# A convolution spectrum's opening in one fixed order of pieces on all engines

## The chip, the core and the metric

The kernel runs on one core of a Trainium2 chip. The metric is the device time of one execution in microseconds, taken as the median over the runs. A core has TensorE (matrix products), VectorE, ScalarE and GpSimd (elementwise work and copies), SyncE (which mainly issues transfers), and 16 DMA engines that move data. Each engine works through its own instructions in order and waits on semaphores. In the profile's lines the engines are PE, DVE, ACT, POOL and SP; PEld is TensorE's loading of stationary operands, and a "q" behind an engine's name is its queue of issued instructions.

## What is computed

The reference runs two kinds of block twice, forward, and then the gradient of everything. Cut to what matters:

```python
def _A_ref(q, k, v, shift_k, ssm_k, ssm_D):          # S = 2048, D = 448, 4 taps
    k_shift = sum(k_pad[:, t:t + S, :] * shift_k[:, ks - 1 - t] for t in range(ks))
    kv = k_shift * v
    y_f = rfft(kv padded to 2S) * rfft(ssm_k padded to 2S)
    y = irfft(y_f)[:S].astype(bfloat16) + kv * ssm_D
    return q * y

def _B_ref(x, w1, w2):                                # 448 -> 1792 -> 448
    return silu(x @ w1) @ w2

x = x + _A_ref(layernorm(x), A_k, A_v, A_shift_k, A_ssm_k, A_ssm_D)
x = x + _B_ref(layernorm(x), B_w1, B_w2)
x = x + _A_ref(...); x = x + _B_ref(...)              # the same operands again
# outputs: x, and the gradients of q, k, v, shift_k, ssm_k, ssm_D, w1, w2 for grad_out
```

The convolution's result `y` depends on k, v and the filter alone, not on x, so it is computed once, ahead of everything else. This part is the opening.

## The kernel before

**The opening** is `_ssm_prefix`. It computes a real Fourier transform of length 4096 in two stages (16 by 256), as matrix products with constant tiles. The filter K goes first: it is transposed from its loaded rows (`k_turn`, L392) and multiplied with the constants `M1sb` (`k_stage1`, L403), with the result in the tile KAB. Then follow the pieces that the change orders anew. Each works on one PSUM tile of 4 KB a partition, of which there are four in turn (tag "A"), and a copy takes it out again:

- k's own rows are transposed into `kT` (L432, four tiles, two copies each).
- K's first-stage result is turned for the second stage: seven groups of 16 blocks; groups 0 to 4 by TensorE (`turn`, helper L225, two 64-row transposes a block), groups 5 and 6 by a transposing DMA on SyncE (L426).
- The short convolution with four taps is 32 products with diagonal tiles (`conv`, L449), in eight parts: halves h of the channels, quarters jq of the time. ScalarE copies a part out (L452), GpSimd stores it (`KS_d`, L454), VectorE multiplies it with v (L455), and TensorE takes it through the first stage (`stage1_kv`, L465, two tiles a part, into `A1kv`).
- K's second stage (`spec_k`, helper L244): 14 chunks of 1024. For each pair of chunks GpSimd issues one store of 512 KB to DRAM (`spec_K`, L474) and four transfers of 128 KB that write the pair into KAB's other half with real and imaginary rows swapped (L282).
- `A1kv` is turned (seven groups, L514, into the tiles ZkvA and ZkvB), and each of 14 chunks goes through the second stage (L244), a store (`spec_KV`, L540), the product with K's spectrum by VectorE (`pab`, L542, which reads both halves of KAB), the inverse second stage (`ps_v`, L253 and L254) and a copy back over `A1kv`.
- The layer norm of the first rows of x (`_ln_steps`, L318 to L326, rows in `x0c`) is done in eight steps in between.

Then `ys` (L563) does the inverse first stage. It reads columns of all chunks, so its first product needs the last copy of `ps_v`. The main part follows, in which TensorE's order is the order of the program.

**What sets the order.** In the opening the framework's scheduler orders each engine's instructions, by the program and its own estimates; a planner (`_Bal.pick`) chooses ScalarE or VectorE for each copy by a running sum of estimated costs. Transfers go in order on the queue that issues them. SyncE's are, in the opening: the loads of the filter, the constants, k, v, x's first rows (L378, `x0c`) and the other constants; the two transposing DMAs on KAB (L426); two transposing DMAs that load w2 turned (`w2T`, L436 and L437, into the memory of `k_n`); the first rows of grad_out (`gb0`, L498). ScalarE issues the loads of w1 and w2 (L528, L529, L534) after its copies of chunks 4 and 7. GpSimd issues the stores and the swaps. Each transfer uses one of eight semaphores of its kind in turn, and waits for the transfer eight before it of that kind.

**Buffers.** ks_kv (the parts of the short convolution) and pab share four buffers. The diagonal tiles lie behind the filter's rows in the memory W2, which ZkvA takes over; ZkvB takes over that of `M1sb` (WX); w1 that of `kT`, w2 that of `v_n`.

Of the kernel before, what the change touches and what calls it, by code (L numbers as in the profile page):

```python
# [17 lines left out]
P = 128  # L18
# [101 lines left out]
KPARTS = [(0, 128), (128, 256), (256, 384), (384, 448)]  # L120

# [125 lines left out]

def _fft_inv_stage2_full(k, pa, pb, B1, ci, psum):
# [6 lines left out]
    _copy(nc, k.bal.pick(1024), B1[:, 8 * ci:8 * ci + 8, :].rearrange("p a b -> p (a b)"), pv[:].rearrange("p a b -> p (a b)"))  # L255
# [56 lines left out]
def _ln_steps(k, pool, c, src, si, n_g):  # L312
# [4 lines left out]
    for tl in range(4):  # L317
        k.tc.keep_in_program_order(nc.vector.bn_stats(out=st[:, tl, :], in_=src(tl)))  # L318
# [6 lines left out]
    for tl in range(4):  # L325
        k.tc.keep_in_program_order(nc.vector.tensor_scalar(out=n_g[:, tl, :], in0=src(tl), scalar1=mv[:, tl, 0:1], scalar2=r[:, tl:tl + 1], op0=ALU.subtract, op1=ALU.mult))  # L326
        yield
# [6 lines left out]
def _ssm_prefix(k):  # L334
# [4 lines left out]
    with ExitStack() as es:  # L339
# [6 lines left out]
        k.M1sb = k.wk.tile([P, 16, 2, P], BF16, name="M1sb", tag="WX")  # L346
# [21 lines left out]
        m1f = k.M1sb[:].rearrange("p a c k -> p (a c k)")  # L368
# [49 lines left out]
        def turn(src, dst, g):  # L418
            pt = psum.tile([P, 2, 16, 64], BF16, name="ps_tr", **a_)
            for i in range(16):  # L420
                _turn64(k, pt, i, src[:, 16 * g + i, :])
            for lo, hi, o in dst(g):
                _copy(nc, bal.pick((hi - lo) * P, dve_ns=0.53), o.rearrange("p i (r x) -> p r i x", r=2), pt[:, :, lo:hi, :])

        for g in range(5, 7):
            nc.sync.dma_start_transpose(out=Z[:, 16 * g:16 * g + 16, :], in_=A1Kf[:, 16 * g:16 * g + 16, :].rearrange("p a b -> p (a b)"))  # L426
        for jq in range(4):
            pt = psum.tile([DC, ND, 4, P], BF16, name="ps_kT", **a_)
            for u in range(4):
                j = 4 * jq + u  # L430
                for dc in range(ND):
                    nc.tensor.transpose(pt[:, dc, u, :], kn[:, j, dc * DC:(dc + 1) * DC], k.ident[:])  # L432
            for e, lo, hi in ((nc.scalar, 0, 2), (nc.vector, 2, 4)):
                _copy(nc, e, kT[:, jq, lo:hi, :, 1:129], pt[:, lo:hi])
        k.w2T = k.wk.tile([P, ND, F], BF16, name="w2T", tag="WY")
        nc.sync.dma_start_transpose(out=k.w2T[:, 0:3, :], in_=k.B_w2[:, 0:384])  # L436
        nc.sync.dma_start_transpose(out=k.w2T[:, 3:4, :], in_=k.B_w2[:, 320:448])  # L437
        DH = D // 2

        def conv(h, jq):  # L440
            ds = slice(h * DH, (h + 1) * DH)
            pc = psum.tile([P, 4, 256], FP32, name="ps_cv", tag="A", bufs=4)
            for u in range(4):
                j = 4 * jq + u
                for e in range(2):
                    for t in range(4):
                        js = (j - t) % J
                        src = kT[:, js // 4, 2 * h + e, js % 4, 1:129] if j >= t else kT[:, js // 4, 2 * h + e, js % 4, 0:128]
                        nc.tensor.matmul(pc[:, u, e * DC:(e + 1) * DC], lhsT=src, rhs=diag[:, 2 * h + e, t, :], start=(t == 0), stop=(t == 3))  # L449
            kk = work.tile([P, 2, 4, DH], BF16, name="ks_kv", tag="pab", bufs=4)  # L450
            ks, kvt = kk[:, 0], kk[:, 1]
            nc.scalar.copy(ks, pc[:, :, :DH])  # L452
            bal.add("act", 0.95)
            nc.gpsimd.dma_start(out=k.KS_d[h, :, 4 * jq:4 * jq + 4, :], in_=ks)  # L454
            nc.vector.tensor_tensor(out=kvt, in0=ks, in1=vn[:, 4 * jq:4 * jq + 4, ds], op=ALU.mult)  # L455
            bal.add("dve", 0.62)
            return kvt

        def stage1_kv(h, jq, kvt):
            for u in range(0, 4, 2):  # L460
                n2 = 4 * jq + u
                ps = psum.tile([P, 2, 2, 256], FP32, name="ps_s1", **k.pt["s1"])
                for w in range(2):
                    for c in range(2):
                        nc.tensor.matmul(ps[:, w, c, :DH], lhsT=k.M1sb[:, n2 + w, c, :], rhs=kvt[:, u + w, :], start=True, stop=True)  # L465
                _copy(nc, bal.pick(4 * DH), A1kv[:, 112 * h:112 * (h + 1), :, n2:n2 + 2, :].rearrange("p b c w s -> p w c b s"),
                      ps[:, :, :, :DH].rearrange("p w c (b s) -> p w c b s", s=2))

        def spec_k(cp):
            for ci in (2 * cp, 2 * cp + 1):  # L470
                o = Ka[:, ci * 1024:(ci + 1) * 1024]
                _copy(nc, bal.pick(1024), o, _fft_stage2_full(k, o, ci, psum)[:])
# [4 lines left out]
        k.na0 = _hd(k, [P, 4, D], "na0")  # L477
        norm = _ln_steps(k, work, 0, lambda tl: k.x0c0[:, tl, :], 0, k.na0)
        prev = []
        for h in range(2):  # L480
            for i, jq in enumerate((1, 2, 3, 0)):
                if len(prev) > 1:
                    stage1_kv(*prev.pop(0))
                prev.append((h, jq, conv(h, jq)))
                next(norm, None)
                bal.add("dve", 0.7)
                if h == 0:
                    for g in (2 * i, 2 * i + 1):
                        if g < 5:
                            turn(A1Kf, lambda g: [(0, 16, Z[:, 16 * g:16 * g + 16, :])], g)  # L490
                else:
                    spec_k(i)
        for p in prev:
            stage1_kv(*p)
        H2 = SPEC // 2
        Zkv = [k.wk.tile([P, H2], BF16, name="ZkvA", tag="W2"), k.wk.tile([P, H2], BF16, name="ZkvB", tag="WX")]
        k.gb0 = _hd(k, [P, 4, D], "gb0")
        nc.sync.dma_start(out=k.gb0[:], in_=_pm(k.grad_out[0])[:, 0:4, :])  # L498
        for i in range(4, 7):
            spec_k(i)  # L500

        B1 = A1kv[:].rearrange("p b c n s -> p (b c n s)").rearrange("p (a x) -> p a x", x=P)

        def zkv(lo, hi):
            h = lo // H2
            return Zkv[h][:, lo - h * H2:hi - h * H2]

        def zdst(g):
            cuts = [(0, 16)] if g != 3 else [(0, 8), (8, 16)]
            return [(lo, hi, zkv(2048 * g + lo * P, 2048 * g + hi * P).rearrange("p (a b) -> p a b", b=P)) for lo, hi in cuts]  # L510
        for g in range(7):
            pt = psum.tile([P, 16, P], BF16, name="ps_tr", **a_)
            for i in range(16):
                nc.tensor.transpose(pt[:, i, :], B1[:, 16 * g + i, :], k.ident[:])  # L514
            for lo, hi, o in zdst(g):
                _copy(nc, bal.pick((hi - lo) * P, dve_ns=0.53), o, pt[:, lo:hi, :])
        hold = []

        def cons_prod(ci, ps):
            sl = slice(ci * 1024, (ci + 1) * 1024)  # L520
            xs = zkv(ci * 1024, (ci + 1) * 1024)
            if ci in (4, 7):
                with tc.issue_after(nc.scalar.copy(xs, ps[:]).ins):
                    if ci == 4:
                        w1x = k.wk.tile([P, ND * F + 2 * D], BF16, name="w1sb", tag="W1")
                        k.w1sb = w1x[:, 0:ND * F].rearrange("p (c f) -> p c f", f=F)
                        k.xq = [w1x[:, ND * F:].rearrange("p (j d) -> p j d", d=D)]
                        nc.scalar.dma_start(out=k.w1sb[:, 0:3, :], in_=k.B_w1[0:384, :].rearrange("(c p) f -> p c f", p=P))  # L528
                        nc.scalar.dma_start(out=k.w1sb[:, 3, :], in_=k.B_w1[320:448, :])  # L529
                    else:  # L530
                        w2x = k.wk.tile([P, (NF + 2) * D], BF16, name="w2sb", tag="WB")
                        k.w2sb = w2x[:, 0:NF * D].rearrange("p (c d) -> p c d", d=D)
                        k.xq.append(w2x[:, NF * D:].rearrange("p (j d) -> p j d", d=D))
# [841 lines left out]
```

## Time and profile before

| | us |
|---|---|
| time, median of 3 runs (lowest to highest) | 702.56 (701.79 to 702.73) |
| time of the profiled execution | 701.8 |
| its span, first to last instruction | 700.0 |
| outside the span | 1.8 |
| TensorE busy over the span | 666.0 (95%) |
| VectorE, ScalarE, GpSimd busy | 484.1, 432.9, 101.3 |
| first `ps_y` (end of the opening) | 90.73 |
| first `pab` | 63.58 |
| first and last swap of KAB issued | 43.0, 66.8 |

The span is the profile's time axis. A busy share is a mean over stages with different limits, so a stage is judged by what its own waits end on. The granted clock of TensorE is 0.998 of full speed over the span.

### The profile page before, as it was taken

Reading aid. Unit: us, or ns where it says so; the run is one execution under the profiler, and the core shown is the slowest. Engines: PE = TensorE matmul, PEld = TensorE weight load, DVE = VectorE, ACT = ScalarE, POOL = GpSimd, SP = SyncE. Lnnn points to the kernel's source line nnn. Section 1 sums busy time; section 2 is a strip of 40 time slices with the busy share of each in tenths; the row PEclk is TensorE's granted clock in tenths of the full one; section 3 lists DMA queues with packets and bytes.
Section 4 is the critical chain, followed back from the end, with each engine's and each line's share of the span. In section 5 each row is a group of like instructions: output and inputs, shape, how many; then the busy total and the mean of one; then the engine's idle time right before and its main releaser. Section 6 shows DMA issues by size and latency. Waiting matters only on the chain.

```text
span 700.0 us, 14553 instructions
## 1 busy us (share of the span) xinstructions
PE 666.0 (95%) x5897; PEld 358.8 (51%) x5933; DVE 484.1 (69%) x1131; ACT 432.9 (62%) x522; POOL 101.3 (14%) x173
## 2 busy tenths in 40 slices
PE   6898789999999999999999999999999999999996
PEld 5876545454444444434444444544554555555664
DVE  6688862676889948899578874853946545538991
ACT  5888766968856857769577585223554553554431
POOL 1057110110011100111000100010111211102311
PEclk9999999999999999999999999999999999999999
DMA  8999938459899976698677799959557888966981
GB/s 321 270 298 306 376 84 210 118 107 243 219 231 249 246 200 166 146 240 221 185 165 194 194 242 329 262 172 229 177 208 280 307 279 307 352 188 215 331 293 42
DMA packets 199798, 161.03 MB, mean 230 GB/s; under 512 B 147698, under 2 KB 180213, under 8 KB 198963
## 3 DMA queue, kind: packets, MB, share of 16 engines
q1 hardware_dynamic: 184550, 111.78, 58.8%
q0 software_dynamic: 10368, 36.29, 15.3%
q10 hardware_dynamic: 4812, 12.04, 5.0%
q8 instruction: 46, 0.75, 0.4%
q14 instruction: 22, 0.17, 0.1%
HBM read 66.05 MB, written 54.60 MB: 172 GB/s over the span
## 4 chain that ended last, share of the span: by engine, by line
PE 57%; DVE 22%; issue 10%; ACT 5%; POOL 3%; DMA 2%; POOLq 0%; DVEq 0%; ACTq 0%
PE ps_d L1046 19%; PE ps_n L836 8%; PE ps_h L638 6%; PE ps_g L638 6%; PE ps_o L798 5%; DVE ln_st L301 2%; DVE lb_v L994 2%; PE ps_v L265 2%; PE ps_cv L449 2%; POOL rstd L306 2%; DVE n L309 1%; DVE lb_v L997 1%; DVE lb_v L998 1%; DVE X L802 1%; PE ps_h L642 1%
## 5 line engine op out<-in xcount | busy, mean ns | idle before, releaser
L1046 PEld LDWEIGHTS <-dstat 128*128 128x128 bf16 x896 | 84.0, 98 | 77.8 <-issue 4.0
L836 PE MATMUL ps_n<-w1T,ghT 128*128 128x448 bf16 x448 | 96.6, 353 | 2.0 <-DVE ghT L821 1.7
L798 PE MATMUL ps_o<-w2sb,aT 128*128 128x448 bf16 x448 | 89.2, 353 | 0.7 <-DVE X L802 0.7
L638 PE MATMUL ps_h<-nT,w1sb 128*128 128x512 bf16 (+1 forms) x410 | 83.5, 336 | 2.2 <-ACT Dall L116 1.0
L116 ACT CAST ghT<-ps_g 128x1024 bf16<-128x1024 f32 (+1 forms) x54 | 48.4, 899 | 58.4 <-PE ps_g L642 47.7
L638 PE MATMUL ps_g<-nT,w2T 128*128 128x512 bf16 x317 | 77.9, 379 | 2.2 <-DVE Dall L117 0.5
L836 PEld LDWEIGHTS <-ghT 128*128 128x128 bf16 x448 | 41.4, 98 | 50.7 <-DVE ghT L821 6.7
L798 PEld LDWEIGHTS <-aT 128*128 128x128 bf16 x448 | 43.2, 98 | 41.1 <-issue 2.8
L638 PEld LDWEIGHTS <-w1sb 128*128 128x128 bf16 x420 | 39.2, 98 | 36.7 <-issue 7.2
L781 ACT ACTIVATE aT<-ps_h 128x1024 bf16<-128x1024 f32 (+1 forms) x48 | 44.2, 921 | 19.4 <-PE ps_h L638 10.5
L116 ACT CAST Dall<-ps_h 128x1024 bf16<-128x1024 f32 (+2 forms) x60 | 54.3, 904 | 0.0
L994 DVE SCALAR_TENSOR_TENSOR lb_v<-lb_u,n 128x448 bf16<-128x448 bf16 x60 | 37.2, 620 | 24.6 <-ACT lb_u L840 24.1
L791 ACT ACTIVATE Dall<-Dall 128x1024 bf16<-128x1024 bf16 (+1 forms) x48 | 53.2, 1186 | 0.1
L638 PEld LDWEIGHTS <-w2T 128*128 128x128 bf16 x336 | 31.3, 98 | 42.1 <-issue 7.2
L306 POOL TENSOR_TENSOR rstd<-ln_ve,mhalf 128x2 f32<-128x2 f32 (+1 forms) x24 | 19.9, 831 | 221.1 <-DVE ln_ve L305 221.1
L1046 PE MATMUL ps_d<-X,dstat 128*128 128x448 bf16 x224 | 47.9, 353 | 0.0
L1046 PE MATMUL ps_d<-go,dstat 128*128 128x448 bf16 x224 | 47.2, 353 | 0.0
L1046 PE MATMUL ps_d<-n3m,dstat 128*128 128x448 bf16 x224 | 46.4, 353 | 0.0
L1046 PE MATMUL ps_d<-n1m,dstat 128*128 128x448 bf16 x224 | 46.3, 353 | 0.0
L840 ACT ACTIVATE lb_u<-ps_n,rstd 128x448 bf16<-128x448 f32 x32 | 20.5, 640 | 28.7 <-PE ps_n L836 24.3
L116 ACT CAST A1g<-ps_v 128x1024 bf16<-128x1024 f32 x14 | 14.9, 1066 | 36.5 <-PE ps_v L265 36.5
L802 DVE TENSOR_TENSOR X<-X,ps_o 128x448 bf16<-128x448 bf16 x32 | 19.5, 610 | 21.3 <-PE ps_o L798 21.1
(206 smaller groups left out, 1111.6 us busy)
## 6 DMA issues: line engine op xcount, KB each, us to landing
dstat<-a_d SPq DMA_DIRECT2D x28, 512.0 KB, 5.0
dstat<-g_d SPq DMA_DIRECT2D x28, 512.0 KB, 5.2
a_d<-turned SPq DMA_DIRECT2D x16, 512.0 KB, 3.0
g_d<-turned SPq DMA_DIRECT2D x16, 512.0 KB, 3.2
a_d<-turned SPq DMA_DIRECT2D x16, 384.0 KB, 2.7
g_d<-turned SPq DMA_DIRECT2D x16, 384.0 KB, 3.0
spec_K<-KAB POOLq DMA_DIRECT2D x7, 512.0 KB, 5.4
KAB<-KAB POOLq DMA_DIRECT2D x28, 128.0 KB, 4.6
```

What stands on the lines that cost most here:

```text
L116: return nc.scalar.copy(out, in_)
L265: nc.tensor.matmul(pv[:, r ^ (ci & 1), i, :], lhsT=src[ri, i * P:(i + 1) * P], rhs=k.Gsb[ri, g, ri], start=first, stop=not first)
L306: nc.gpsimd.tensor_tensor(out=r[:, lo:hi], in0=ve[:, lo:hi], in1=k.mhalf[:, lo:hi], op=ALU.pow)
L638: self.nc.tensor.matmul(ps, lhsT=w[:, b, ft * P:(ft + 1) * P], rhs=x[:, b], start=(start and b == 0), stop=(stop and b == bs[2]))
L781: self.last_silu = nc.scalar.activation(aT[hh][:, o:o + hi - lo, :], ps(lo, hi), ACT.Silu)
L791: self.nc.scalar.activation(dT[hh][:, o:o + n, :], dT[hh][:, o:o + n, :], ACT.Derivative_silu)
L798: nc.tensor.matmul(po[:, :D], lhsT=aT[ft // 7][:, ft % 7, tl * P:(tl + 1) * P], rhs=self.w2sb[:, ft, :], start=(ft == 0), stop=(ft == NF - 1))
L802: self.last_o = nc.vector.tensor_tensor(out=X[:, t, :], in0=X[:, t, :], in1=po[:, :D], op=ALU.add)
L836: nc.tensor.matmul(pn[:, :D], lhsT=gh[ft // 7][:, ft % 7, tl * P:(tl + 1) * P], rhs=self.w1T[:, ft, :], start=(ft == 0), stop=(ft == NF - 1))
L840: nc.scalar.activation(u0[:], pn[:, :D], ACT.Identity, scale=k.rstd[2 * L + 1][:, t:t + 1], accum_out=cp[:, tl, 0:1])
L994: nc.vector.scalar_tensor_tensor(out=v[:], in0=u0, scalar=-1.0 / D, in1=n_t, op0=ALU.mult, op1=ALU.mult, accum_out=cp[:, 1:2])
L1046: self.nc.tensor.matmul(ps[:, :D], lhsT=st[:, t, :], rhs=mov[:, t, :], start=(first and t == 0), stop=(last and t == NT - 1))
```

## The change

All pieces from k's turn on (T) get one written order, the string OPENING, and the scheduler is switched off for all five engines there. Every engine gets its instructions in the string's order. A piece's first letter is its kind, then its numbers (chunk, group, or h, jq and u); capital letters are TensorE's work, small letters the copies of its result, with the engine at the end (a for ScalarE, d for VectorE) and x or y for the first or second part of a tile that is copied in two.

| letters | piece |
|---|---|
| T, t | k's transposes, and copies to kT |
| K, k | turn of K's groups 0 to 4, now 16 transposes of 128 by 128 a group |
| C, c, m | short convolution; copy on ScalarE and store KS_d; product with v on VectorE |
| S, s | first stage of kv |
| P, p, Q | K's second stage; store and four swaps of a pair of chunks |
| Z, z | turn of A1kv's groups 0 to 6, on TensorE |
| F, f | second stage of kv, with the stores spec_KV |
| M, V, v | product with K's spectrum on VectorE; inverse second stage; copy |
| N | one step of the layer norm |
| W | loads on SyncE: 0 gb0, 1 w2T, 2 w1, 3 w2 |

Further: chunks of kv are no longer taken in rising order; gb0 is loaded ahead of w2T; w1 and w2 are loaded from SyncE instead of ScalarE; the parts of the short convolution get two buffers of their own and pab three (four shared before); the diagonal tiles move behind `M1sb`, so that ZkvA is free earlier; the inverse second stage's helper returns its tile instead of copying it.

```diff
+OPENING = """
+W0 T3 N0 T0 t3ya t3xd T1 t0xd t0ya N1 T2 t1xa t1yd C00 t2xa t2yd N2 C03 c00 N3 m00 K4 c03 N4 S001 k4d S000 s001a K1 m03
+s000a P8 k1d P9 p8a S031 N5 P3 p9a s031d P2 p3a P10 Q4 p2d P11 p11a C01 p10d Q1 N6 S030 c01 N7 C02 s030a m01 P12 c02 P13
+p12d Q5 S010 p13a S011 m02 K2 s010a s011d S020 S021 s020a k2d K0 Q6 s021a P5 k0d P4 p5a Z1 p4d P1 P0 p1a z1d Q2 C10 p0a
+C13 c10 Q0 m10 S101 c13 S100 s101d Z2 s100a m13 Z0 z2d S131 S130 s131a z0d K3 s130a k3d F0 F1 f0a F2 f1d P7 f2a P6 M0
+C11 p7a M1 p6a C12 c11 Q3 M2 F5 m11 c12 F3 f5d S111 f3a S110 m12 F4 s111a V0 s110d f4a S121 M3 S120 W1 W2 W3 v0a V1
+s120d s121a V2 M4 v1a Z4 v2a M5 Z5 Z6 z5a z4d Z3 z6d F9 z3ya F10 z3xd F12 f9a f10d F13 f12a F6 f13d F8 f6a F11 f8d V3
+f11a V4 M13 v3a V5 v4a M12 V13 v5a M9 V12 v13a M8 V9 v12a F7 M10 V8 f7a M11 V10 v9a v10a M7 V11 v8a M6 V7 v11a v7d V6
+v6a
+"""
...
-        w2o = k.wk.tile([P, 2 * S + ND * 4 * DC], BF16, name="ksd", tag="W2")
+        w2o = k.wk.tile([P, 2 * S], BF16, name="ksd", tag="W2")
...
-        diag = w2o[:DC, 2 * S:].rearrange("p (c j d) -> p c j d", c=ND, j=4)
+        diag = m1t[:DC, 16 * 2 * P:].rearrange("p (c j d) -> p c j d", c=ND, j=4)
...
-            kk = work.tile([P, 2, 4, DH], BF16, name="ks_kv", tag="pab", bufs=4)
+            live["m", h, jq] = work.tile([P, 2, 4, DH], BF16, name="ks_kv", tag="kk", bufs=2)
...
-            pab = work.tile([P, 2, 1024], BF16, name="pab", tag="pab", bufs=4)
+            pab = work.tile([P, 2, 1024], BF16, name="pab", tag="pab", bufs=3)
...
+        def transposes(key, name, src, g):
+            pt = bank(key, [P, 16, P], name, BF16)
+            for i in range(16):
+                nc.tensor.transpose(pt[:, i, :], src[:, 16 * g + i, :], k.ident[:])
+        def Q(cp):
             lo, hi = cp * 2048, (cp + 1) * 2048
             nc.gpsimd.dma_start(out=k.SPEC_d["K"][:, lo:hi], in_=Ka[:, lo:hi])
             _swap_halves_dma(k, KAB[:, 0, :], Ka, lo, hi)
...
+        def W(i):
+            if i == 0:
+                nc.sync.dma_start(out=k.gb0[:], in_=_pm(k.grad_out[0])[:, 0:4, :])
+            elif i == 1:
+                k.w2T = k.wk.tile([P, ND, F], BF16, name="w2T", tag="WY")
+                nc.sync.dma_start_transpose(out=k.w2T[:, 0:3, :], in_=k.B_w2[:, 0:384])
+                nc.sync.dma_start_transpose(out=k.w2T[:, 3:4, :], in_=k.B_w2[:, 320:448])
+            elif i == 2:
...
+                nc.sync.dma_start(out=k.w1sb[:, 0:3, :], in_=k.B_w1[0:384, :].rearrange("(c p) f -> p c f", p=P))
+                nc.sync.dma_start(out=k.w1sb[:, 3, :], in_=k.B_w1[320:448, :])
             else:
...
+                nc.sync.dma_start(out=k.w2sb, in_=k.B_w2.rearrange("(c p) d -> p c d", p=P))
+        two = {"P", "p", "F", "f", "M", "V", "v"}
+        with tc.manual_schedule(engines={e.engine for e in (nc.tensor, nc.scalar, nc.vector, nc.gpsimd, nc.sync)}):
+            for g in range(5, 7):
+                nc.sync.dma_start_transpose(out=Z[:, 16 * g:16 * g + 16, :], in_=A1Kf[:, 16 * g:16 * g + 16, :].rearrange("p a b -> p (a b)"))
+            for tok in OPENING.split():
...
+                do[kind](*args)
```

The instructions behind the opening stand in the same order on every engine as before, but for one copy of the first layer's rows on VectorE that changes places with its neighbours.

More of the change, by code (lines that the diff above doesn't have):

```diff
@@ L427, in _ssm_prefix, with zkv @@
-        for jq in range(4):
-            pt = psum.tile([DC, ND, 4, P], BF16, name="ps_kT", **a_)
+        DH = D // 2
+        H2 = SPEC // 2
+        B1 = A1kv[:].rearrange("p b c n s -> p (b c n s)").rearrange("p (a x) -> p a x", x=P)
+        Zt = [None, None]
+        def zkv(lo, hi):
+            h = lo // H2
+            if Zt[h] is None:
+                Zt[h] = k.wk.tile([P, H2], BF16, name=("ZkvA", "ZkvB")[h], tag=("W2", "WX")[h])
+            return Zt[h][:, lo - h * H2:hi - h * H2]
@@ L429, in _ssm_prefix, with T @@
+        def T(jq):
+            pt = bank(("t", jq), [DC, ND, 4, P], "ps_kT", BF16)
             for u in range(4):
-                j = 4 * jq + u
                 for dc in range(ND):
[L432 to L442, printed above, removed]
+                    nc.tensor.transpose(pt[:, dc, u, :], kn[:, 4 * jq + u, dc * DC:(dc + 1) * DC], k.ident[:])
+        def t(jq, part, eng):
+            lo = 2 * part
+            _copy(nc, eng, kT[:, jq, lo:lo + 2, :, 1:129], live["t", jq][:, lo:lo + 2])
@@ L443, in conv, with K, k_, C @@
+        def K(g):
+            transposes(("k", g), "ps_tr", A1Kf, g)
+        def k_(g, part, eng):
+            _copy(nc, eng, Z[:, 16 * g:16 * g + 16, :], live["k", g][:])
+        def C(h, jq):
+            pc = bank(("c", h, jq), [P, 4, 256], "ps_cv")
             for u in range(4):
@@ L452, in conv @@
-            nc.scalar.copy(ks, pc[:, :, :DH])
-            bal.add("act", 0.95)
-            nc.gpsimd.dma_start(out=k.KS_d[h, :, 4 * jq:4 * jq + 4, :], in_=ks)
[L455 to L472, printed above, removed]
+                    for tt in range(4):
+                        js = (j - tt) % J
+                        src = kT[:, js // 4, 2 * h + e, js % 4, 1:129] if j >= tt else kT[:, js // 4, 2 * h + e, js % 4, 0:128]
+                        nc.tensor.matmul(pc[:, u, e * DC:(e + 1) * DC], lhsT=src, rhs=diag[:, 2 * h + e, tt, :], start=(tt == 0), stop=(tt == 3))
@@ new lines, in c, with m, S_ @@
+        def c(h, jq):
+            live["m", h, jq] = work.tile([P, 2, 4, DH], BF16, name="ks_kv", tag="kk", bufs=2)
+            ks = live["m", h, jq][:, 0]
+            nc.scalar.copy(ks, live["c", h, jq][:, :, :DH])
+            nc.gpsimd.dma_start(out=k.KS_d[h, :, 4 * jq:4 * jq + 4, :], in_=ks)
+        def m(h, jq):
+            kk = live["m", h, jq]
+            nc.vector.tensor_tensor(out=kk[:, 1], in0=kk[:, 0], in1=vn[:, 4 * jq:4 * jq + 4, h * DH:(h + 1) * DH], op=ALU.mult)
+        def S_(h, jq, u):
+            ps = bank(("s", h, jq, u), [P, 2, 2, 256], "ps_s1")
+            for w in range(2):
+                for cc in range(2):
+                    nc.tensor.matmul(ps[:, w, cc, :DH], lhsT=k.M1sb[:, 4 * jq + 2 * u + w, cc, :], rhs=live["m", h, jq][:, 1, 2 * u + w, :], start=True, stop=True)
@@ new lines, in s, with P_, p @@
+        def s(h, jq, u, part, eng):
+            n2 = 4 * jq + 2 * u
+            _copy(nc, eng, A1kv[:, 112 * h:112 * (h + 1), :, n2:n2 + 2, :].rearrange("p b c w s -> p w c b s"),
+                  live["s", h, jq, u][:, :, :, :DH].rearrange("p w c (b s) -> p w c b s", s=2))
+        def P_(ci):
+            live["p", ci] = _fft_stage2_full(k, Ka[:, ci * 1024:(ci + 1) * 1024], ci, psum)
+        def p(ci, part, eng):
+            _copy(nc, eng, Ka[:, ci * 1024:(ci + 1) * 1024], live["p", ci][:])
@@ L475, in spec_k @@
             _swap_halves_dma(k, KAB[:, 0, :], Ka, lo, hi)
[L477 to L506, printed above, removed]
@@ L517, in _ssm_prefix @@
-        hold = []
-        def cons_prod(ci, ps):
-            sl = slice(ci * 1024, (ci + 1) * 1024)
-            xs = zkv(ci * 1024, (ci + 1) * 1024)
[L522 to L533, printed above, removed]
-                        nc.scalar.dma_start(out=k.w2sb, in_=k.B_w2.rearrange("(c p) d -> p c d", p=P))
-                bal.add("act", 1.4)
-            else:
-                _copy(nc, bal.pick(1024), xs, ps[:])
-            if ci in (1, 3, 5, 6, 8, 10, 12, 13):
-                lo = (ci - (ci not in (6, 13))) * 1024
-                nc.gpsimd.dma_start(out=k.SPEC_d["KV"][:, lo:(ci + 1) * 1024], in_=zkv(lo, (ci + 1) * 1024))
-            pab = work.tile([P, 2, 1024], BF16, name="pab", tag="pab", bufs=4)
-            nc.vector.tensor_tensor(out=pab[:], in0=xs.rearrange("p (o f) -> p o f", o=1).broadcast_to((P, 2, 1024)), in1=KAB[:, :, sl], op=ALU.mult)
-            bal.add("dve", 1.25)
-            hold.append((pab[:, 1], pab[:, 0], ci))
-            if len(hold) > 2:
-                pa, pb, cj = hold.pop(0)
-                _fft_inv_stage2_full(k, pa, pb, B1, cj, psum)
@@ L549, in _ssm_prefix, with D_, Z_, z @@
-        for ci in range(NCI):
-            cons_prod(ci, _fft_stage2_full(k, zkv(ci * 1024, (ci + 1) * 1024), ci, psum))
-        for pa, pb, cj in hold:
-            _fft_inv_stage2_full(k, pa, pb, B1, cj, psum)
+        def D_(g):
+            nc.sync.dma_start_transpose(out=block(g), in_=B1[:, 16 * g:16 * g + 16, :].rearrange("p a b -> p (a b)"))
+        def Z_(g):
+            transposes(("z", g), "ps_tr", B1, g)
+        def z(g, part, eng):
+            lo, hi = (8 * part, 8 * part + 8) if g == 3 else (0, 16)
+            _copy(nc, eng, block(g, lo, hi), live["z", g][:, lo:hi, :])
@@ new lines, in F_, with f @@
+        def F_(ci):
+            live["f", ci] = _fft_stage2_full(k, zkv(ci * 1024, (ci + 1) * 1024), ci, psum)
+        def f(ci, part, eng):
+            _copy(nc, eng, zkv(ci * 1024, (ci + 1) * 1024), live["f", ci][:])
+            seen.add(ci)
+            for lo, hi in ((0, 2), (2, 4), (4, 6), (6, 7), (7, 9), (9, 11), (11, 13), (13, 14)):
+                if ci in range(lo, hi) and seen >= set(range(lo, hi)):
+                    nc.gpsimd.dma_start(out=k.SPEC_d["KV"][:, lo * 1024:hi * 1024], in_=zkv(lo * 1024, hi * 1024))
@@ new lines, in M, with V, v @@
+        def M(ci):
+            pab = work.tile([P, 2, 1024], BF16, name="pab", tag="pab", bufs=3)
+            xs = zkv(ci * 1024, (ci + 1) * 1024)
+            nc.vector.tensor_tensor(out=pab[:], in0=xs.rearrange("p (o f) -> p o f", o=1).broadcast_to((P, 2, 1024)), in1=KAB[:, :, ci * 1024:(ci + 1) * 1024], op=ALU.mult)
+            live["V", ci] = pab
+        def V(ci):
+            pab = live["V", ci]
+            live["v", ci] = _fft_inv_stage2_full(k, pab[:, 1], pab[:, 0], ci, psum)
+        def v(ci, part, eng):
+            _copy(nc, eng, B1[:, 8 * ci:8 * ci + 8, :].rearrange("p a b -> p (a b)"), live["v", ci][:].rearrange("p a b -> p (a b)"))
```

56 lines of the change are left out of this document (29 added, 27 removed).

## The prediction

> **What bounds the kernel now.** I read the busy time by stretch first. TensorE is 95% busy over the span, but the opening, the first 90 us, is the exception:
>
> ```profile
> 50.00:60.00 10.00, 9.28 (x106) 7.03 (x106) 9.35 (x10) 8.26 (x9) 8.20 (x17) 1.00 0.95 303
> 60.00:70.00 10.00, 7.98 (x110) 6.32 (x108) 8.59 (x9) 9.01 (x10) 6.62 (x13) 1.00 0.98 308
> 80.00:90.00 10.00, 6.44 (x116) 5.26 (x115) 6.49 (x6) 6.35 (x7) 1.30 (x3) 1.00 0.95 356
> ```
>
> After the stretch stand its length, then busy time of TensorE, weight loads, VectorE, ScalarE and GpSimd, the granted clock, the DMA share and GB/s. The clock is full (1.00), the DMA engines are 95 to 98% busy, and TensorE waits. The chain of waits in order of time (start, length, what) says for whom:
>
> ```profile
> 63.58 1.24 DVE pab L542
> ...
> 86.98 1.24 DVE pab L542
> ...
> 89.36 1.24 DVE A1kv L117
> ...
> 90.73 0.93 PE ps_y L563 x4
> ```
>
> The opening ends when VectorE's last copy of `ps_v` ends, at 90.6; `ps_y` follows at once and needs all of it. From the first `pab` to there are 27.0 us. VectorE's own work in that time is 14 `pab` at 1.14 (three in a row took 3.50, one 1.22), three copies of `ps_s` at 1.14 and two of `ps_v` at 1.14: 21.7 us, so it waits 5.3. After 90 us TensorE is nearly full and nothing has a fixed date, so I let a shift of the opening's end pass to the end one for one.
>
> `pab` also needs KAB's swapped half, which GpSimd's queue makes. Its timeline (start, length, instruction, idle time before it):
>
> ```profile
> 42.47 0.54 POOL L474 DMA_DIRECT2D spec_K<-KAB  x1 [1.54 <-DVE KAB L117]
> 43.00 1.97 POOL L282 DMA_DIRECT2D KAB<-KAB  x4
> ...
> 63.72 0.97 POOL L282 DMA_DIRECT2D KAB<-KAB  x2 [0.69 <-DMA spec_K<-KAB]
> ```
>
> One store and four swaps make a piece Q of 1 MB. Before, the seven Q go in the order 0 to 6 from 42.47; the first `pab` needs only the first, and the last swap of the sixth is issued at 64.2 (second of the pair). SyncE's timeline and the DMA view in three windows show what shares the engines with this stream. q1 is SyncE's queue, q0 GpSimd's (packets, MB, share of 16 engines):
>
> ```profile
> 30.16 6.52 SPq L436 DMA_TRANSPOSE w2T<-in_B_w_dram  x1
> 36.72 2.52 SPq L437 DMA_TRANSPOSE w2T<-in_B_w_dram  x1
> 39.28 1.21 SPq L498 DMA_DIRECT2D gb<-in_grad_out_dram  x1
> ```
>
> From 33.6 to 37.6:
>
> ```profile
> q1 hardware_dynamic: 4229, 1.08, 119.4%
> ```
>
> From 37.6 to 41:
>
> ```profile
> q1 hardware_dynamic: 1171, 0.29, 107.3%
> q0 software_dynamic: 63, 0.23, 27.2%
> ```
>
> From 45 to 60:
>
> ```profile
> q0 software_dynamic: 1539, 4.90, 96.0%
> ```
>
> Alone, w2T's transposes move 0.27 MB/us (0.289 in their steady part) and fill the engines; alone, the stream moves 0.329. Together, in the second window, both move 158 GB/s: neither engine time nor bytes simply add up. The KS_d stores issued from 33 to 41 needed 6.2 to 7.2 us to land, while all eight have a median of 5.1 and a least of 3.5:
>
> ```profile
> DMA to landing us min/median/max: 6.2/6.7/7.2
> ```
>
> Before, w2T was through when the stream began. That is what the change takes away.
>
> **Parts that cost nothing.** K's turn with whole 128-square transposes: 16 instead of 32 a group (33 small ones took 0.65, so 0.52 a group), now 0.89 as for L514; 5 x 0.37 = 1.9 us more TensorE, covered by TensorE's waits for copies. Two copies of turned K go from ScalarE (1.88) to VectorE (1.21). TensorE's idle 2.27 us at 27.6, with no releaser ("issue"), may go or stay: in the new order TensorE is ahead of the copies there. The weights leave ScalarE, where casts ran 0.91 apart across their issue, so nothing is won. On SyncE w1sb waits for the last C, w2sb for the last m; landing took 11.9 to 17.0, so with C12 near 62 and m12 near 69 they are there by 76 and 86, ahead of their first uses in L638 at 102 and L798 at 112. w2T is written late in the string but is not late: SyncE issues it as soon as gb0's 1.21 us is over, since it waits only for k_n's transposes. The convolution's spectrum was turned by TensorE before too.
>
> **The new path, in four terms.** *First Q.* VectorE's fixed list puts N0 first, which needs x0c: issued at 7.82, landing 15.5 later, 23.3. Behind this wait stand all of VectorE's pieces, and TensorE's C00 behind t3 and t0. Then N0 to N3 (0.76 each, and 0.2), four t copies (0.61 each): 5.7, 29.0. GpSimd's power 1.04, N4 0.31, k4 1.21, P8 0.59, p8 and p9 0.91 and 1.03 on ScalarE: the first Q (Q4) at 34.2. That is 8.3 earlier than before.
>
> *Stream to the sixth Q.* The order is 4 1 5 6 2 0 3, and the first `pab`, M0, needs Q0: the sixth. Before, from 42.5 to the landing of the sixth's last swap: issue 64.2, swaps land in 3.4 to 4.6, so 68.2: 25.7 us, with three KS_d stores in between, as now. M0 at 59.9 if nothing disturbs it.
>
> *w2T beside it.* w2T starts 1.2 us later than before, its packets at about 34.8. The first data of the stream move some 3 us after their issue, at 37. By then 2.2 us x 0.289 = 0.65 MB of w2T are through, of 1.34 and 0.45 MB: 1.1 MB go beside the stream. The trace has no such overlap of this length, so I bound it. If engine time adds up, it costs w2T's own 1.1/0.289 = 3.9 us. If both go as in the second window, w2T needs 1.1/0.085 = 13 us, in which the stream moves 0.068 instead of 0.329 MB/us: 10.2 lost. If gaps in the stream take w2T, 0; less than nothing is excluded, as no transfer is taken out of that time. I take 4.0, near the adding-up value, since w2T's second piece between 42 and 44 ran beside a store at 338 GB/s in all, without loss. M0 at 63.9. [...]
>
> *From M0 to the end.* VectorE has this queued behind M0: 14 M x 1.14, m11 and m12 0.53 each, s110 and s120 1.0 each, z4 and z6 1.13 each, z3 0.60, four f and v7 1.14 each: 27.6 us, 5.9 more than before. M3 waits for V0 (a pab buffer, now three instead of four), and small waits: 1.3. Sum 28.9. ScalarE has less to do after M0, and its c12 waits for a KS_d store (two buffers instead of four) that lands about when M0 starts: covered, as m12 stands behind M2, m11 and f5.
>
> 34.2 + 25.7 + 4.0 + 28.9 = 92.8, against 90.6: 2.2 us later. The profiled execution took 701.8 for its span of 700.0, so 704.0 on its own scale; the median of the runs is 702.56, so **704.8**.
>
> **Rivals.** [...]
>
> *Faster: w2T goes through the stream's gaps.* The stream is paced by GpSimd's issue (2.5 us a Q) and by waits for earlier DMAs; if these gaps take w2T, the third term is 0, and the end 88.8: 700.8. It decides in this direction if w2T costs the stream under 1.8 us, that is if M0 starts before 61.7. For it: the first Q is 8.3 earlier. Against: 96% share from 45 to 60, hardly a gap.
>
> *Heavy mixing.* The second window's rates hold for all of w2T: 10.2, end at 99.0, 711.0. Against: 42 to 44.
>
> **How the numbers follow.** Chances: forecast 0.48, turns 0.22, gaps 0.18, heavy 0.12. A difference under 0.2% (1.4 us) can hardly be measured here. The forecast's own spread (third term 3 to 6.5) gives 703.8 to 707.3, so 0.40 of it slower and 0.08 the same; turns 0.15 same, 0.04 faster, 0.03 slower; gaps 0.13 faster, 0.05 same; heavy slower. Faster 0.17, same 0.28, slower 0.55. The range of 700.6 to 708.6 leaves out most of heavy and the low edge of gaps.
>
> **What would show it.** M0 near 64, released by a DMA of KAB, with VectorE idle for several us before it; the first store of spec_K at about 34; KAB and KS_d DMAs issued between 34 and 45 landing after 6 us and more; C00 held to 25.5 by VectorE's wait for x0c; 29 us from M0 to the last A1kv. I am wrong if M0 starts before 61.7, if M0 is not the late one, or if the time after `ps_y` differs.

## The result, and the profile after

The changed kernel takes 711.60 us (median of 6 runs, 709.41 to 715.58), the kernel before 702.67 (median of 6): the ratio is 1.0134, 95% interval 1.0103 to 1.0165. It is slower by 9 us. The profiled execution took 709.41, its span is 707.6. The prediction said 704.8 and gave 708.6 as the upper end.

The chain of waits of the changed kernel (start, length, what):

```profile
64.23 4.33 DMA KAB<-KAB
...
69.82 2.35 DVE pab L540 x2
...
96.80 1.02 ACT A1kv L116
97.86 0.64 PE ps_t L645 x32
98.51 0.88 PE ps_y L593 x4
```

The opening ends at 97.8 instead of 90.6. From the first `ps_y` to the end it is 609.1 us after (707.6 less 98.5) and 609.3 before (700.0 less 90.73): all that is lost is lost in the opening. VectorE's timeline (start, length, instruction, idle time before it and what ended it) has the first `pab`, M0:

```profile
68.68 3.50 DVE L540 TENSOR_TENSOR pab<-ZkvA,KAB 128x2048 bf16<-128x2048 bf16 x3 [2.95 <-DMA KAB<-KAB]
```

Before it started at 63.58, and the prediction had 63.9. From M0 to the last copy of `ps_v` it is 29.1 us, as predicted (28.9). So the loss lies ahead of M0, and GpSimd's timeline shows where:

```profile
36.24 0.54 POOL L514 DMA_DIRECT2D spec_K<-KAB  x1 [3.99 <-DVE A1kv L117]
...
42.42 0.49 POOL L294 DMA_DIRECT2D KAB<-KAB  x1 [2.01 <-DMA spec_K<-KAB]
43.64 0.49 POOL L294 DMA_DIRECT2D KAB<-KAB  x1 [0.73 <-DMA KAB<-KAB]
44.16 1.13 POOL L489 DMA_DIRECT2D KS_d<-ks_kv  x2
51.01 0.54 POOL L514 DMA_DIRECT2D spec_K<-KAB  x1 [5.73 <-issue]
```

The stream begins at 36.24 and stops after two pieces: the swap at 42.42 waits 2.01 us for the store of 36.24, the transfer eight before it, and the store at 51.01 comes after 5.73 us of idle time, when the swap issued at 38.25, again eight before it, has landed. That is at 50.49, 12.2 us after its issue; w2T's second part lands at 51.45. The DMA view of the stretch from 44 to 51 (MB, share of 16 engines, then an issue group with its median us to landing):

```profile
q0 software_dynamic: 267, 0.91, 78.4%
q1 hardware_dynamic: 992, 0.25, 33.0%
...
KS_d<-ks_kv POOLq DMA_DIRECT2D x2, 224.0 KB, 11.4
```

The engines are occupied (111% in sum) and move 165 GB/s; a packet of the stream takes 0.784 x 16 x 7/267 = 0.33 us instead of 0.96 x 16 x 15/1539 = 0.150 (kernel before, 45 to 60), one of w2T 0.037 instead of 1.194 x 16 x 4/4229 = 0.018 (kernel before, 33.6 to 37.6). The busy time by stretch (columns as in the prediction) has the consequence:

```profile
44.00:51.00 7.00, 6.92 (x105) 5.79 (x105) 4.46 (x4) 4.54 (x5) 1.26 (x3) 1.00 1.11 165
51.00:57.00 6.00, 0.00 (x0) 0.00 (x0) 0.41 (x1) 1.34 (x2) 4.07 (x8) 0.75 0.98 317
57.00:69.00 12.00, 11.55 (x138) 9.80 (x139) 6.87 (x8) 7.69 (x9) 7.87 (x16) 0.84 0.98 317
```

From 51 to 57 TensorE does nothing at all: on ScalarE a copy of the convolution waits 6.30 us for a buffer whose KS_d store is one of the two that took 11.4.

```profile
55.66 1.71 ACT L488 CAST ks_kv<-ps_cv 128x896 bf16<-128x896 f32 x2 [6.30 <-DMA KS_d<-ks_kv]
```

What met the stream is little more than the second of w2T's two transposing DMAs. The packets of the first were through at 39.5, just after the stream's first packets had moved (39.2). The second, 0.46 MB, took from 41.6 to 49.7; from 41 to 44 w2T's queue shows

```profile
q1 hardware_dynamic: 842, 0.21, 78.2%
```

and 157 GB/s in all.

### The profile page after: what moved, and what is told of

Its sections match the earlier page's. It is cut to its first block, busy times and chain, and to the rows that moved or that the text cites. A ratio compares the mean times of both kernels' runs of the same rounds, so it can differ in the third digit from the quotient of the medians.

```text
span 707.6 us, 14393 instructions
## 1 busy us (share of the span) xinstructions
PE 671.7 (95%) x5817; PEld 364.0 (51%) x5853; DVE 485.3 (69%) x1132; ACT 429.7 (61%) x521; POOL 101.7 (14%) x173
## 4 chain that ended last, share of the span: by engine, by line
PE 54%; DVE 22%; issue 11%; DMA 5%; ACT 4%; POOL 4%; POOLq 0%; SPq 0%; DVEq 0%; ACTq 0%
PE ps_d L1076 18%; PE ps_n L866 8%; PE ps_h L668 6%; PE ps_g L668 6%; PE ps_o L828 5%; DVE ln_st L313 2%; DMA x0c<-in_A_q_dram 2%; DVE lb_v L1024 2%; PE ps_v L277 2%; POOL rstd L318 2%; DVE n L321 1%; DVE lb_v L1027 1%; DVE lb_v L1028 1%; DVE X L832 1%; PE ps_h L672 1%
## 5 line engine op out<-in xcount | busy, mean ns | idle before, releaser
L828 PEld LDWEIGHTS <-aT 128*128 128x128 bf16 x448 | 43.2, 98 | 41.1 <-issue 2.7
L668 PEld LDWEIGHTS <-w1sb 128*128 128x128 bf16 x420 | 39.2, 98 | 36.7 <-issue 7.2
```

What stands on the lines that cost most here:

```text
L668: self.nc.tensor.matmul(ps, lhsT=w[:, b, ft * P:(ft + 1) * P], rhs=x[:, b], start=(start and b == 0), stop=(stop and b == bs[2]))
L828: nc.tensor.matmul(po[:, :D], lhsT=aT[ft // 7][:, ft % 7, tl * P:(tl + 1) * P], rhs=self.w2sb[:, ft, :], start=(ft == 0), stop=(ft == NF - 1))
```

## The experiments

Theory A: w2T's transposing DMAs and GpSimd's stream hinder each other, and this makes Q0, and so M0, late. Theory B: the two buffers of ks_kv make the convolution wait for KS_d stores. Theory C: it is the place of Q0, sixth in the stream. A further question was why the stream starts at 36.24 and not at 34.2. In the string `OPENING`, W1 is w2T, W2 and W3 are the loads of w1 and w2, N a step of the norm.

**e1_w2T_last**

```
- ... S120 W1 W2 W3 v0a ...
+ ... S120 W2 W3 W1 v0a ...
```

> The changed kernel with one edit: SyncE issues w2T's two transposing DMAs after w2sb instead of right after gb0, so about 70 instead of 29.8 and 37.6; their first use is at 104. Theory A (the transposes mix with GpSimd's stream and starve it between 44 and 50): the fourth swap, issued at 38.25, lands in under 7 us instead of 12.24, no KS_d store takes over 8 us, Q0's last swap lands at 60 to 62 instead of 68.56, M0 starts then, the copies of ps_v end near 90; 702 (701 to 704). Theory B (two buffers for ks_kv: the next convolution copy waits for the KS_d store of two pieces before, and this holds TensorE): the stores wait less, but if the buffers were the reason the 6 us of idle TensorE near 51 stay in part; 706 to 708. Theory C (the place of Q0 in the order, not w2T): M0 stays at 67 or later; 709 to 712.

Measured: 714.94 us (713.51 to 718.25), ratio 1.0164 (1.0146 to 1.0182). The opening behaved as A says: swaps landed in 4.1 to 6.3 us, and VectorE's timeline has

```profile
62.22 3.50 DVE L540 TENSOR_TENSOR pab<-ZkvA,KAB 128x2048 bf16<-128x2048 bf16 x3 [3.67 <-DMA KAB<-KAB]
```

M0 comes 25.4 us after the first store (36.87), 6.5 earlier than in the changed kernel, which rules out C as the whole of it. But the time went up, since w2T met other transfers: SyncE's timeline and, below it, the chain of waits.

```profile
68.37 29.56 SPq L558 DMA_TRANSPOSE w2T<-in_B_w_dram  x1
97.97 10.76 SPq L559 DMA_TRANSPOSE w2T<-in_B_w_dram  x1
```

```profile
87.68 22.65 DMA spec_KV<-ZkvB
110.55 0.64 DVE X L715
```

The last store of spec_KV took 22.65 us; X takes over its buffer and waits until 110. The expectation of 702 overlooked these stores: moving the transposes moved the collision.

**e2_three_ks**

```
- live["m", h, jq] = work.tile([P, 2, 4, DH], BF16, name="ks_kv", tag="kk", bufs=2)
+ live["ks", h, jq] = work.tile([P, 4, DH], BF16, name="ks", tag="ks", bufs=3)
+ live["m", h, jq] = work.tile([P, 4, DH], BF16, name="kv", tag="kk", bufs=2)   # in m()
```

> The changed kernel with one edit: the convolution's output and its product get tiles of their own, three buffers for the stored ks and two for the product, instead of two buffers for both together. w2T stays where it is. Theory A: ScalarE's wait of 6.30 us for a KS_d store at 55.66 shrinks or goes and TensorE's idle 6 us near 51 shrinks, but Q0's last swap still lands at 68 to 69 and M0 starts then; 709 to 712, no change. Theory B: M0 and the end come 4 to 6 us earlier; 705 to 707. Theory C: as A.

Measured: 717.10 us, ratio 1.0202 (1.0182 to 1.0222), slower than any theory had it. M0 came only at 75.47. In this execution w2T landed at 53.80 and the third piece's store was issued at 53.53 (51.01 in the changed kernel), and there is a second collision, in the chain of waits:

```profile
65.78 9.57 DMA KAB<-KAB
```

Q0's last swap took 9.57 us beside w1sb, which was issued at 65.66; the swaps issued just before took 6.4 to 6.5. w1sb waits only for the last C, and with buffers to spare C came earlier than the swap. B as the main cause is not borne out: the stream stopped again behind its own unlanded transfers, and M0 waited for a swap and not for the convolution. The test is a weak one, since the wait for a KS_d store shrank only from 6.30 to 5.20 us and a second one of 3.57 came up.

**e3_w2T_plain**

```
- nc.sync.dma_start_transpose(out=k.w2T[:, 0:3, :], in_=k.B_w2[:, 0:384])
+ nc.sync.dma_start(out=k.w2T[:, 0:3, :], in_=k.B_w1[0:384, :].rearrange("(c p) f -> p c f", p=P))
  (and the fourth block likewise)
```

> The changed kernel with w2T's two transposing DMAs replaced by two plain DMAs of the same bytes, tile, queue and place (they load w1, so the second product's weights are not w2 turned: this leaves the turn out). Theory A with the transposing as the cause: 1.8 MB of plain loads add up with the stream, 1.1 to 1.8 MB at 0.329 MB/us make 3.4 to 5.5 us on an undisturbed Q0 at 60.5, so M0 at 62 to 66; 703 to 707. Theory A with any second queue as the cause: M0 stays at 67 to 69; 709 to 712. Theories B and C: M0 within 1.5 us of 68.7.

This kernel leaves out the turn of w2. Measured: 705.95 us (704.01 to 708.33), ratio 1.0042 (1.0029 to 1.0055). As many bytes on the same queue at the same place, not turned, land at 39.25 instead of 51.45; the DMA view from 37.6 to 41 has both queues side by side at 376 GB/s:

```profile
q0 software_dynamic: 275, 0.90, 75.9%
q1 hardware_dynamic: 117, 0.35, 25.5%
```

M0 starts at 62.78, 26.2 us after the first store, against 25.4 with no w2T there (e1) and 32.4 in the changed kernel. So the plain load costs the stream 0.8 us and the transposing one 7.0: A, with the transposing as the cause. Two things go with the turn and are not separated from it here. The plain load was nearly through when the stream came (at most 0.35 MB beside it). And its packets are larger: 0.35 MB in 117 packets against 0.25 MB in 992, that is 3.0 KB against 0.25. The rest of the order is still slower than the kernel before.

**e4_w2T_last_norm_later** (e1, and)

```
- W0 T3 N0 T0 t3ya t3xd T1 t0xd t0ya N1 T2 ... t2yd N2 C03 c00 N3 m00 K4 c03 N4 S001 k4d ...
+ W0 T3 T0 t3ya t3xd T1 t0ya t0xd T2 ... t2yd N0 C03 c00 N1 m00 K4 c03 N2 S001 k4d N3 S000 ... S031 N4 ... N5 ...
```

> As e1_w2T_last, and the layer norm's eight steps are moved later in VectorE's fixed list, so that the wait for x0c (landing 22.9) no longer stands at its head, and kT's two halves are copied by ScalarE first, then VectorE, for each piece. Theory A: the first store of spec_K is issued 3 to 4 us earlier than 36.24, so near 32.5 to 33, M0 at 57 to 58.5, the end 3 us before e1; 698.5 (697 to 700.5). If x0c's wait costs nothing because TensorE's convolutions or the copies set the first Q anyway, the same as e1, within 1 us.

Measured: 712.03 us, ratio 1.0129 (1.0114 to 1.0145); against e1 the first store comes 5.4 us earlier (31.47), M0 5.3 (56.89) and the last copy of `ps_v` 6.6 (86.03, where the kernel before has 90.59). The end of it is eaten by w2T, as in e1. The stretch from 80 to 90 (busy time) and its DMA view:

```profile
80.00:90.00 10.00, 6.01 (x109) 5.04 (x106) 5.23 (x6) 5.51 (x6) 0.54 (x1) 0.84 1.21 123
```

```profile
q1 hardware_dynamic: 1035, 0.26, 75.8%
q0 software_dynamic: 267, 0.95, 44.0%
```

From 80 to 100 w2T's transposes and five stores moved 0.63 and 2.00 MB. At their rates alone (0.289 and 0.329 MB/us) that is 2.2 and 6.1, together 8.3 us; it took 20, and w2sb, the only other load of that time, had landed at 80.35. This is the clearest view of A.

**e5_kept_apart**

```
+ def B(i): nc.gpsimd.tensor_copy(fz[:], k.w2T[0:1, 2:4, 0:1])
  order: e4's, W1 behind T2, pieces 0 and 4 exchanged, B0 ahead of the first Q,
  Q in the order 0 1 2 6 4 5 3, W2 behind v4a and W3 behind v12a on nc.scalar
```

> The changed kernel with its order rewritten so that w2T never shares the DMA engines with much else: the norm's steps later (as e4_w2T_last_norm_later), w2T first on SyncE after the turns of KAB, a one-element copy on GpSimd that reads w2T and so holds the stream until it has landed, the pieces 0 and 4 of k exchanged and the stream in the order in which the products need it (0 1 2 6 4 5 3), w1sb and w2sb issued late from ScalarE. Theory A (transposing DMAs and the stream starve each other, and whatever the opening saves reaches the end one for one): w2T lands at 40 to 42, the first store of spec_K follows, swaps land in 4 to 6 us, M0 waits for the copies of ps_s and not for a DMA and starts at 54 to 57, the last copy of ps_v ends at 83 to 86, and the end is 609.7 later: span 693 to 696, 697 (695 to 700). Rival (the late stream only moves the wait to the later products): M9, M10 or M7 wait for KAB's swaps, the last copy at 89 or later, 701 or more.

Measured: 701.35 us (697.83 to 705.14), ratio 0.9988 (0.9963 to 1.0012). M0 is at 55.47, as A had it, but the stream began only at 45.45 (w2T landed at 44.86 even with the stream held away), and the last copy came at 88.06. The chain of waits has two places that neither theory named, and the spec_KV stores again:

```profile
55.09 5.61 DMA KS_d<-ks_kv
...
76.81 1.94 ACTq L570
...
82.84 10.04 DMA spec_KV<-ZkvB
```

A KS_d store, late behind the held stream, holds c12's buffer (B, as a second-order cause); the issue of w1sb's second part takes ScalarE's queue 1.94 us; and beside the loads a spec_KV store takes 10.04 us.

**e6_first_piece_only** (labels 0 and 4 of k's pieces exchanged, nothing else)

> The changed kernel with one edit: the labels 0 and 4 exchanged in the tokens of k (turn, copy, spectrum, store and swaps), so that the stream goes 0 1 5 6 2 4 3 and the first product needs its first piece instead of its sixth. w2T stays beside the stream. Theory C (the place of Q0): M0 comes at 62 or earlier and the end 6 to 8 us earlier than the changed kernel; 703 to 705. Theory A with B behind it: the starved stores of KS_d still hold the convolution's copies (two buffers) and TensorE, so M0 comes only at 62 to 66; 705 to 708.

Measured: 709.05 us, ratio 1.0092 (1.0071 to 1.0113), little better than the changed kernel. M0 no longer waits for a DMA but starts at 67.54, later than expected: in this execution swaps needed up to 15.8 us, and w2T landed at 55.95. The late transfers reach the products by the convolution's buffers as well (a copy on ScalarE waits 7.46 us for a KS_d store before 57.39), so exchanging the pieces alone does not get round them.

**e7_not_apart** (e5 without B0)

> As e5_kept_apart without the one-element copy, so the stream starts near 38 while w2T is still moving. Theory A: w2T lands 4 to 12 us later than in e5_kept_apart, the first swaps land 8 us or more after their issue, KS_d's stores wait too, and the end is 3 to 8 us later than e5_kept_apart: 700 to 705. If mixing is not what costs, the earlier start of the stream makes it equal or 1 us faster.

Measured: 698.71 us (697.98 to 699.95), ratio 0.9944 (0.9927 to 0.9960): faster than the kernel before by 4 us, and faster than e5, against A's number. The stream starts at 40.14, w2T lands at 46.50, swaps take 4.9 to 6.8 us. The strong form of A, that mixing is worse than waiting, falls here. More than that: the second transposing DMA of w2T ran beside the KS_d stores and the stream's first store, and the DMA view from 41 to 44 has

```profile
q1 hardware_dynamic: 1730, 0.44, 65.3%
q0 software_dynamic: 151, 0.55, 48.3%
```

Together that is 332 GB/s, and a packet of w2T takes 0.653 x 48/1730 = 0.018 us, as when it is alone. In the changed kernel the same part needed 8.1 us, at 157 and then 165 GB/s. So a transposing DMA beside other transfers was not slow each time; no run shows what decides it. What still costs is in the chain of waits:

```profile
81.19 9.00 DMA spec_KV<-ZkvB
90.41 0.64 DVE X L720
```

**e8_before_whole_turn**

```
- for i in range(16): _turn64(k, pt, i, src[:, 16 * g + i, :])
+ for i in range(16): nc.tensor.transpose(pt[:, i, :], src[:, 16 * g + i, :], k.ident[:])
```

> The kernel before with one part of the change alone: k's five turns by TensorE with 16 transposes of 128 by 128 instead of 32 of 64 rows. The prediction put 1.9 us more on TensorE, all of it beside its waits: same, within 0.7 us of the kernel before. If TensorE is the limit in the stretch from 25 to 45, it is 1 to 2 us slower.

Measured: 702.48 us, ratio 0.9996 (0.9983 to 1.0008). The turn by whole squares cost nothing here.

**e9_stream_held** (the changed kernel with B0 ahead of Q4)

> The changed kernel with one edit: a one-element copy on GpSimd that reads w2T stands ahead of the first store of spec_K, so the stream starts only when w2T has landed. Order, places and buffers as in the changed kernel. Theory A: w2T lands at 41 to 44 instead of 51.45, the stream starts 5 to 8 us later than 36.24, but its swaps land in 4 to 5 us and Q0's last lands 25 us after the start, at 66 to 69: M0 no later than the changed kernel's 68.7, and 706 to 710. If engine time simply adds up, w2T's 1.1 MB beside the stream cost the same wherever they move, and holding the stream idles the engines at first: M0 2 to 4 us later than 68.7, 712 to 715.

Measured: 715.74 us, ratio 1.0185 (1.0168 to 1.0202). GpSimd's timeline:

```profile
44.69 0.18 POOL L556 COPY fz<-w2T 1x2 bf16<-1x2 bf16 x1 [11.90 <-DMA w2T<-in_B_w_dram]
45.19 0.54 POOL L514 DMA_DIRECT2D spec_K<-KAB  x1 [0.33 <-issue]
```

The stream starts 9.0 us later than in the changed kernel, takes 27.4 us to M0 instead of 32.4, and M0 is at 72.62, 3.9 later. Holding is worse than mixing, as the second branch had it. So the 7.0 us are not all loss by mixing. With the stream away w2T still landed only at 44.54, 5.3 us after the changed kernel's stream moved its first packets (39.2). And w2T was slow for a while with nothing beside it; the only packets from 41 to 43 are

```profile
q1 hardware_dynamic: 555, 0.14, 136.9%
```

This is 70 GB/s, with 0.079 us a packet instead of 0.018. How the 7.0 divide into w2T's own time and the mixing stays open: e9's w2T had 0.79 MB left at 39.2, the changed kernel's 0.54.

**e10_weights_around** (e7 with W2 behind v1a and W3 behind v6a)

> As e7_not_apart, with the two weight loads moved on ScalarE: w1sb after the second copy of ps_v (near 63) instead of near 75, w2sb after the last copy of ps_v (near 85) instead of near 78. In e7_not_apart the last stores of spec_KV, issued beside these loads, took 9 to 10 us to land, and X, which takes their buffer, waited for them until 90.4, 5 us after the last copy of ps_v. Theory A (whatever the opening saves reaches the end, unless another transfer of the opening is made late): the stores land in 3 to 6 us, X starts near 86.5, and the end is 3 to 4 us earlier: 694 to 697. Rival: w1sb now slows the pieces Q5 and Q3 and the products M10 or M7 wait for them; 697 to 700.

Measured: 699.12 us, ratio 0.9941 (0.9926 to 0.9956), the same as e7. The last five spec_KV stores landed in 5 to 6 us and X waited for none, as A had it; but w1sb made the swaps of Q5 and Q3 take up to 12, Q3's last landed at 82.76, M7 followed at 82.88, and the last copy of `ps_v` came at 87.42 instead of 85.48. Both theories' mechanisms are there, and about cancel.

**e11_weights_three_ks** (e10 with e2's buffers)

> As e10_weights_around, with three buffers for ks and two for the product instead of two for both (as e2_three_ks). Theory B as a second-order cause: convolution copies no longer wait for KS_d stores, c10 and c13 come 1 to 3 us earlier, M0 is 0 to 1.5 us earlier, 0 to 2 us faster than e10_weights_around. If M0's date is set by TensorE and the copies alone, no change within 0.7 us.

Measured: 699.41 us, ratio 0.9957 (0.9943 to 0.9971): no difference from e10 (699.12). M0 55.75 against 55.56. In this order, where the stream is not starved, the buffers did not matter.

**e12_plain_first_piece** (e3 with e6's exchange)

> As e3_w2T_plain (w2T's place filled by plain loads, the turn of w2 left out), with the labels 0 and 4 of k's pieces exchanged as in e6_first_piece_only. Theory C without the starvation: M0 no longer waits for a swap, starts 2 to 4 us earlier than the 62.8 of e3_w2T_plain, and the time falls by 1.5 to 3.5 us, to 702.5 to 704.5. If the convolution's copies and not Q0 are the next limit, the same as e3_w2T_plain within 0.7 us.

Measured: 701.19 us, ratio 0.9975 (0.9962 to 0.9988), 4.8 below e3, more than C had (the turn of w2 is left out here too). M0 starts at 57.92 instead of 62.78. So the place of Q0 is worth 4.9 us where w2T's transposes are away. With them (e6) M0 came only 1.1 us earlier, in an execution whose w2T landed 4.5 later.

## Why the prediction was wrong

The chain was the predicted one: Q4's store, the stream to Q0, M0 released by a swap of KAB, 29 us of VectorE's list, `ps_y`, and nothing behind it changed. Three steps were right: the stream undisturbed (25.7 predicted, 25.4 in e1 and e4), the time from M0 on (28.9, 29.1; e1, e3 and e9, with the same list, show 30.4 to 30.6), and the parts that cost nothing, as far as they were tried (e8 for the turn). C00 started at 25.0, as its wait for x0c had it (25.5).

Wrong were the sizes of two terms and the step to the median:

- *First Q.* 34.2 predicted, 36.24 measured: 2.0 us. x0c landed at 22.9, near enough, and VectorE's wait for it was there. Left out was that it also holds ScalarE. The two engines copy halves of the same `kT` piece and wait for one another; ScalarE's timeline:

```profile
24.99 2.84 ACT L116 COPY kT<-ps_kT 112x1024 bf16<-112x1024 bf16 x3 [2.14 <-DVE kT L117]
```

  e4 shows what the head of the list costs in all: with the norm behind the copies, and ScalarE's half first, the first Q is 5.4 us earlier than in e1. Of the 2.0 us, 1.2 are there when N3 ends (30.2, predicted 29.0); the rest are GpSimd's power (1.29, predicted 1.04) and small steps behind it.
- *w2T beside the stream.* 4.0 predicted, 32.4 less 25.4 = 7.0 measured: the mis-sized term, 3 us. Two errors in it offset one another, and that 4.0 came as near as it did is luck. The prediction put 1.1 MB beside the stream. It was half: w2T's packets began at 32.7 and not at 34.8, the stream's at 39.2 and not at 37, and 0.54 MB were left. And its price was too low by far. At w2T's own 0.289 MB/us 0.54 MB make 1.9 us; at the rates of heavy mixing they make 0.54/0.085 = 6.4, in which 0.79 of the stream is lost, 5.0; measured are 7.0, above both (the two figures are estimates from these rows).

  The low price came from a misread stretch. I took 42 to 44 in the kernel before for w2T beside a store, at 338 GB/s without loss. But from 43.2 on that queue's packets are those of gb0's plain load; the view of the kernel before from 43 to 45 has them at 2 KB on the mean, where w2T's are 0.25:

```profile
q1 hardware_dynamic: 228, 0.47, 63.6%
```

  Where w2T itself ran beside a store, from 42 to 43, the two moved 300 GB/s together (0.14 and 0.16 MB), each about half of its own rate: engine time added up, for one microsecond, and it was not without loss. The stretch in which both together moved 158 was the better measure. e3 shows that the transposing load is what costs, and e4 that mixing can cost by itself. e7 shows the same part beside other transfers at 332 GB/s, so why it was slow in the changed kernel stays open.
- *The median.* I carried 0.8 us from profiled run to median, as before. After, the profiled run was the fastest of six, and the median lies 2.2 above it: 1.4 us. w2T's landing differs from execution to execution where it mixes (51.45, 53.80 and 55.95 in the changed kernel, e2 and e6, which load it alike), and that may be the spread; but e12, without w2T's transposes, spreads over 4.3 us too, and no run settles it.

Sum: 36.2 + 25.4 + 7.0 + 29.1 = 97.7; the miss of 6.8 in the median is 2.0 from the first term, 2.7 from the stream (7.0 and 25.4 against 4.0 and 25.7), 1.4 from the median, and the rest small waits and rounding.

Of the rivals, *turns*, 0.22 in the chances, is a mechanism that no run shows: how an engine chooses between two queues is in no trace. What the runs show is that the packets of both took twice their time from 44 to 51 (0.33 instead of 0.150 us, 0.037 instead of 0.018). *Faster* was wrong in more than its condition: with w2T's transposes out of the way (e3) the end came at 93.4 and not at the 88.8 of the sum, because the first Q was late and the time from M0 grew to 30.6. *Heavy mixing* was the nearest in mechanism. In e4 the two together stay near its 158 GB/s for 20 us (123, then 143), with a smaller part for w2T (0.026 and 0.037 MB/us instead of 0.085). Plain (e3) and transposing (the changed kernel), as many bytes at the same place in the queue landed at 39.25 and at 51.45.

## What to carry to other kernels

Do not price a transposing DMA beside another queue's transfers by its bytes or by its time alone: ask of every place it could go what else moves there (e1), and measure, since a stretch of its own cost more here (e9, 715.74 us against 711.60) and the same part beside other transfers was once as quick as alone (e7, 0.018 us a packet). Before a stretch of a trace serves as evidence, see whose packets they are (2 KB for gb0, 0.25 for w2T). In an order written by hand, look for a step that waits for a late load: N0, waiting for x0c, held VectorE's list and, through the shared `kT` piece, ScalarE for 2.14 us; put it where its input has long landed (e4, with ScalarE's half copied first: 5.4 us). Let pieces travel in the order in which they are used (e12, 4.9 us). e7, which does the last two and starts its stream when most of w2T is through, beats the kernel before by 0.56%.

## What the runs showed of the hardware that I had not expected

A transposing DMA that was held up occupied the queue that issued it: SyncE's issue of w2T's first part lasted 37.8 us in e4 (behind w2sb, which landed at 80.35, and beside stores), 6.5 in the kernel before, and w2T's second part behind it on SyncE was issued only then. Packets of both queues lengthened in that company: in e4's stretch from 80 to 90 those of w2T to 0.758 x 160/1035 = 0.117 us, six times their 0.018, those of the stores to 0.440 x 160/267 = 0.26, and the total fell to 123 GB/s while the engines show 121% busy; in e7's stretch from 41 to 44 w2T's did not (332 GB/s, 0.018 us), and in e9's from 41 to 43 w2T's lengthened with nothing beside them (0.079 us). And the changed kernel's granted clock was 1.00 from 44 to 51, 0.75 from 51 to 57, when TensorE stood still, 0.84 in the 12 us after, and 1.00 again from 69 on; its lower mean clock (0.994 against 0.998) comes with the wait and not before it, and the time behind `ps_y` is the same (609.1 and 609.3).
